# Crossbar transposes of softmax tiles: one per tile from 16 long rows, with the transposed tile kept in groups of 8 queries

## The chip, the core and the metric

The kernel runs on one NeuronCore of a Trainium2 chip. The metric is the device time of one execution in microseconds (us). The engines are TensorE (PE in the rows; PEld is its weight load), VectorE (DVE), ScalarE (ACT), GpSimd (POOL) and SyncE (SP), which here only issues DMAs.

## What is computed

Attention in which each row of scores keeps only what lies within `tau` of its maximum, and behind it a gated feed-forward layer with a three-tap convolution over the tokens:

```
q, k, v: (8, 8, 576, 64) float32;  x: (8, 576, 512) after the heads are joined
scores = q @ k^T / 8;  keep where scores >= max - tau;  attn = softmax(kept)
x = attn @ v
h = relu(x @ w_in)                         # 512 -> 1024
gate = sigmoid(three-tap convolution of h over the tokens)
out = (h * gate) @ w_out                   # 1024 -> 512
```

## The kernel before

**Tiling.** The 8 batches are cut into chunks of 256 and 320 tokens, 16 chunks in all; in a chunk the 8 heads are worked as four pairs of heads. A unit is one tile of 128 query rows (64 queries by two heads, or a leftover tile) against all 576 keys. Each unit computes scores on TensorE (`ps_s`, L569), the row maximum on VectorE (L581), the exponential on ScalarE (L588), the mask on VectorE (L591) and the normalisation on GpSimd (L629). The result is the tile `em`, 128 rows by 1152 float32.

**Two ways to transpose a tile.** The product with v wants `em` with the keys on the partitions, in the tile `eT`. For 53 of the units TensorE transposes blocks of 128 columns into PSUM (`ps_t`, L688) and ScalarE copies them into `eT` (L698 and L704). The other 91 units, all from the second batch on, go through the DMA crossbar (`cross`): ScalarE and GpSimd split the float32 words of `em` into their low and high 16 bits (`parts`, L337 and L339), SP writes `parts` to a DRAM buffer (`rows`, L666), and two DMA transposes per unit, one for each half of 64 queries, read `rows` and write `eT` (L673).

**The layout of eT before.** `eT` is `[128, 5, 9, 64]`: five groups of 64 queries, in each nine steps of keys, in each 64 queries side by side. There are two such buffers, and the two pairs of heads of one `attend` hold both; so the transposes for the next `attend` wait until the matmuls of this one have read them.

**attend** (L711 to L738) multiplies by v: nine steps, in each four matmuls whose moving operand is `eT[on, :w // D, step, :]` (`pa`, L724), `w` being 256 or 320 queries. There are 32 such groups of matmuls, 28 of them reading crossbar output. ScalarE and VectorE carry the result into `x` (L732, L735), on which the feed-forward layer works: `ph` (L754), a gate on ScalarE and VectorE, and `po` (L805). All these are full matmuls, 128 by 128; `ps_s` and `pa` are matmuls of 64 rows by 64 columns, four of which share the array.

**What sets the order.** No engine chooses at run time. `Plan.run` (L121) simulates all operations with a cost in ns for each, a priority, latencies and a cost for a change of the kind of matmul on TensorE (`SWITCH`, L46), and writes each engine's instructions in the order in which the simulation started them. An operation that `cross` declares with other costs or in another number can therefore move instructions on every engine. SP takes its DMAs strictly in the written order.

Of the kernel before, what the change touches and what calls it, by code (L numbers as in the profile page):

```python
# [10 lines left out]
F32 = mybir.dt.float32  # L11
# [4 lines left out]
U16 = mybir.dt.uint16  # L16
AF = mybir.ActivationFunctionType
# [37 lines left out]
FAR = 5  # L55
# [5 lines left out]
ETB = 2  # L61
# [3 lines left out]
LATE = {'load': 1357.0, 'copy': 18200.0, 'rows': 335.0, 'turn': -47.0}  # L65
# [22 lines left out]
class Plan:  # L88
# [13 lines left out]
    def op(self, engine, ns, fn, w=(), r=(), ahead=0.0, other=None, kind=None, late=0.0, port=False, ring=0.0):  # L102

        i = len(self.ops)
        before = set()
        for x in r:
            before.update(self.wrote[x])
            self.read.setdefault(x, set()).add(i)  # L110
        for x in w:
            before.update(self.wrote.get(x, ()))
            before.update(self.read.pop(x, ()))
            self.wrote[x] = (i,)
        before.discard(i)
        bufs = {x[0] for x in (*w, *r)}
        for x in bufs:
            x.left += 1
        self.ops.append((((engine, ns), *(other or ())), self.rank - ahead, fn if other is not None else lambda e: fn(), before, bufs, kind, late, port, ring))
# [135 lines left out]
def tile_tau_attention_gated_ffn(  # L255
# [13 lines left out]
    nc = tc.nc  # L269
    P = 128  # L270
    B, NP, _, _, S = qd.shape
    D = 64
# [4 lines left out]
    NBLK = 2 * S // P  # L277
# [6 lines left out]
    for b in range(B):  # L284
        for tiles in FIRST if not b else GROUPS:
# [4 lines left out]
                b=b, tiles=tiles, new=(o, end - o), cols=(a0, end - a0), tokens=(k0, (end if end == S else end - 1) - k0),  # L290
# [6 lines left out]
    wk = ctx.enter_context(tc.tile_pool(name="wk", bufs=2))  # L297
    sm = ctx.enter_context(tc.tile_pool(name="sm", bufs=4))
    far = ctx.enter_context(tc.tile_pool(name="far", bufs=FAR, space=bass.MemoryType.DRAM))
# [3 lines left out]
    plan = Plan()  # L303
# [49 lines left out]
    def act(n, psum=False):  # L353
        return n * 0.833 + (58 if psum else 95)
# [290 lines left out]
    def cross(u, em, dsts):  # L645

        parts = plan.buf(wk, "stage", STB, [P, 2 * S], U32, f"parts_{u}")

        def halves():
            return parts[:].bitcast(U16).rearrange("p (j k) -> p j k", j=2)  # L650

        rows = plan.buf(far, "rows", FAR, [2 * P, 2 * S], U16, f"rows_{u}")
        a = AHEAD["s"]
        for j in range(2):
            def part(e, j=j):
                src = em[:].bitcast(U16).rearrange("p (k two) -> p two k", two=2)[:, j]
                copy(e, halves()[:, j], src)

            choice = {"act": act(2 * S), "pool": pool1(2 * S), "dve": dve(2 * S)}
            home = ("act", "pool")[j]  # L660
            op(
                home, choice[home], part, w=[(parts, j)], r=[(em, 0), (em, 1)], ahead=a + AHEAD["parts"], port=True,
                other=[(e, ns) for e, ns in choice.items() if e != home]
            )
        put(
            864, lambda: nc.sync.dma_start(rows[:].rearrange("(q two) k -> q two k", two=2), halves()),  # L666
            w=[(rows, 0)], r=[(parts, 0), (parts, 1)], ahead=a, late=LATE["rows"]
        )
        for j in range(2):
            eT, g = dsts[j]  # L670

            def turn(j=j, eT=eT, g=g):
                nc.sync.dma_start_transpose(eT[:].bitcast(U16)[:, g], rows[j * P:(j + 1) * P, :])  # L673

            op("sp", 1560, turn, w=[(eT, (g, "x"))], r=[(rows, 0)], ahead=a, late=LATE["turn"], ring=1650)

    def transposes(u, em, dsts):

        def group(b0, n):

            pt = plan.buf(ps_t, "ps_t", 2, [P, 512], F32, f"ps_t_{u}_{b0}")

            def turns():
                for i in range(n):
                    block = em[:, (b0 + i) * P:(b0 + i + 1) * P]
                    nc.tensor.transpose(out=pt[:, i * P:(i + 1) * P], in_=block, identity=ident[:])  # L688

            op("pe", n * P * 0.852, turns, w=[(pt, 0)], r=[(em, 0), (em, 1), (ident, 0)], ahead=AHEAD["t"], kind="turn")  # L690

            def source():
                return pt[:, :n * P].rearrange("p (b g n) -> p g b n", b=n, g=2)

            if dsts[0][0] is dsts[1][0]:
                (eT, g), _ = dsts
                op(
                    "act", act(n * P, True), lambda: nc.scalar.activation(eT[:, g:g + 2, b0:b0 + n, :], source(), AF.Copy),  # L698
                    w=[(eT, (g, b0))], r=[(pt, 0)], ahead=AHEAD["t"] + AHEAD["evac"]
                )  # L700
            else:
                for j, (eT, g) in enumerate(dsts):
                    op(
                        "act", act(n * D, True), lambda j=j, eT=eT, g=g: nc.scalar.activation(eT[:, g, b0:b0 + n, :], source()[:, j], AF.Copy),  # L704
                        w=[(eT, (g, b0))], r=[(pt, 0)], ahead=AHEAD["t"] + AHEAD["evac"]
                    )

        for b0 in range(0, NBLK, BLOCKS):
            group(b0, min(BLOCKS, NBLK - b0))

    def attend(of, w, parts):  # L711

        pas = [plan.buf(ps_t, "ps_t", 2, [P, 512], F32, f"pa_{i}") for i, *_ in of]
        a = AHEAD["a"]
        read = parts + [(y[3], 0) for y in of]

        for step in range(NBLK):
            def mm(step=step):  # L720
                for (_, p, eT, vt, *_), pa in zip(of, pas):
                    for h in range(2):
                        j, on = h ^ p % 2, slice(h * D, (h + 1) * D)
                        nc.tensor.matmul(  # L724
                            pa[j * D:(j + 1) * D, :w], lhsT=vt[on, step, :], rhs=eT[on, :w // D, step, :],
                            start=(step == 0), stop=(step == NBLK - 1)
                        )

            op("pe", w * 4 / 2.4 + 6, mm, w=[(pa, 0) for pa in pas], r=read, ahead=a, kind="rows")
        for (i, p, eT, vt, x, off), pa in zip(of, pas):  # L730
            def high(pa=pa, x=x, off=off):
                nc.scalar.activation(x[:, 0, off:off + w], pa[:, :w], AF.Copy)  # L732

            def low(pa=pa, x=x, off=off):
                nc.vector.tensor_tensor(x[:, 1, off:off + w], pa[:, :w], x[:, 0, off:off + w].bitcast(F32), op=ALU.subtract)  # L735

            op("act", act(w, True), high, w=[(x, 0)], r=[(pa, 0)], ahead=a + AHEAD["low"])
            op("dve", dve(w), low, w=[(x, 1)], r=[(pa, 0), (x, 0)], ahead=a + AHEAD["low"])  # L738
# [121 lines left out]
    for now in range(len(units) + 1):  # L860
        plan.rank = float(now)
        if now < len(units):
# [4 lines left out]
            both = [i, i + 1] if n is None else [i]  # L867
            for x in both:
                if x not in eTs:
                    eTs[x] = plan.buf(wk, "eT", ETB, [P, 5, NBLK, D], F32, f"eT_{x}")  # L870
            if n is None:
                last = lasts[i]
                sides = [
# [96 lines left out]
```

## Time and profile before

| | |
|---|---|
| median of 3 runs | 833.04 us (832.44 to 833.35) |
| span of the profiled execution, first to last instruction | 832.4 us |
| TensorE busy | 810.5 us, 97% |
| VectorE, ScalarE, GpSimd busy | 722.3 (87%), 610.5 (73%), 496.4 us (60%) |
| granted TensorE clock | 1.000 of full speed throughout |
| share of 16 DMA engines of SP's queue | 76.5% |

Of the profiled execution the span alone is known; it lies 0.6 us under the median of the runs, and sums below are made on the span and carried to the median by that 0.6 us. Matmuls are pipelined and their ends are modelled, so TensorE's time is best read from the starts of its instructions, not from their lengths. A window row gives busy time with the number of instructions in brackets.

### The profile page before, as it was taken

How to read it: one execution, taken by the hardware profiler on the slowest of the kernel's cores; microseconds unless marked ns; L12 is line 12 of the kernel's file. 1: busy time of each engine (PE TensorE's matmuls, PEld its weight loads, DVE VectorE, ACT ScalarE, POOL GpSimd, SP SyncE). 2: the span in 40 equal slices, each digit the busy share in tenths (PEclk: the TensorE clock that was granted, in tenths of full speed). 3: DMA queues.
4: the chain of work that ended last, by engine and by line, in shares of the span. 5: the costliest groups of instructions: out<-in, count | busy, mean ns of one | idle time of the engine just before them, and what ended most of it. 6: DMA issues, size and time to landing. Idle time of an engine off the chain costs nothing.

```text
span 832.4 us, 20658 instructions
## 1 busy us (share of the span) xinstructions
PE 810.5 (97%) x7521; PEld 590.7 (71%) x7521; DVE 722.3 (87%) x1801; ACT 610.5 (73%) x1231; POOL 496.4 (60%) x639
## 2 busy tenths in 40 slices
PE   5899999999999999999999999999999999999998
PEld 2456667777677677767777677767778677777896
DVE  6999999989898799988989789997989979996542
ACT  5999787778777677877776777876767867776642
POOL 3477666855657466764666646774666647665321
PEclk9999999999999999999999999999999999999999
DMA  7544348899889878799998887889888988787200
GB/s 268 183 152 152 91 120 250 189 296 249 233 216 223 218 215 198 202 272 238 183 214 247 231 215 200 222 208 252 221 209 199 249 214 190 208 221 189 50 26 38
DMA packets 266133, 165.49 MB, mean 199 GB/s; under 512 B 220464, under 2 KB 239152, under 8 KB 266032
## 3 DMA queue, kind: packets, MB, share of 16 engines
q1 hardware_dynamic: 265600, 163.87, 76.5%
q8 instruction: 60, 0.98, 0.5%
q14 instruction: 41, 0.34, 0.1%
q10 hardware_dynamic: 432, 0.30, 0.1%
HBM read 47.34 MB, written 63.11 MB: 133 GB/s over the span
## 4 chain that ended last, share of the span: by engine, by line
PE 91%; ACT 4%; DVE 3%; POOL 1%; issue 1%; DMA 0%; POOLq 0%; DVEq 0%
PE ph L754 25%; PE po L805 25%; PE ps_s L569 19%; PE pa L724 16%; PE ps_t L688 6%; ACT em L588 1%; ACT eT L698 1%; DVE few L581 1%; DVE em L591 1%; POOL em L629 1%; POOL stage_f L402 1%; DMA k<-in_kp_dram 0%; DVE t L769 0%; ACT stage_f L389 0%; ACT w1h L410 0%
## 5 line engine op out<-in xcount | busy, mean ns | idle before, releaser
L629 POOL TENSOR_SCALAR em<-em,few 128x576 f32<-128x576 f32 x286 | 232.2, 823 | 182.2 <-DVE few L615 151.3
L588 ACT ACTIVATE em<-ps_s,few 128x576 f32<-128x576 f32 x288 | 209.9, 750 | 79.1 <-DVE few L581 64.1
L581 DVE TENSOR_REDUCE few<-ps_s 128x1 f32<-128x576 f32 x288 | 210.0, 748 | 42.6 <-PE ps_s L569 41.1
L591 DVE SCALAR_TENSOR_TENSOR em<-ps_s,few,em 128x576 f32<-128x576 f32 x288 | 224.1, 810 | 11.8 <-ACT em L588 4.9
L754 PE MATMUL ph<-x,w1h 128*128 128x322 f32 (+1 forms) x1024 | 232.4, 305 | 0.0
L754 PEld LDWEIGHTS ph<-x,w1h 128*128 128x128 f32 x1024 | 171.1, 189 | 23.2 <-issue 17.9
L344 POOL TENSOR_TENSOR gl<-t,gh 128x255 fp32r<-128x255 f32 (+9 forms) x192 | 121.3, 642 | 111.1 <-ACT gh L784 105.1
L569 PE MATMUL ps_s<-k,q 64*64 64x288 f32 x2048 | 164.6, 423 | 9.0 <-DVE k L341 4.3
L724 PE MATMUL pa<-eT,v 64*64 64x256 f32 (+1 forms) x2304 | 155.3, 404 | 0.7 <-ACT eT L698 0.7
L754 PE MATMUL ph<-x,w1l 128*128 128x322 f32 (+1 forms) x512 | 151.1, 295 | 0.0
L724 PEld LDWEIGHTS pa<-eT,v 64*64 64x64 f32 x2304 | 95.3, 133 | 47.5 <-issue 2.3
L805 PE MATMUL po<-w2h,gh 128*128 128x512 f32 x288 | 119.4, 415 | 0.0
L569 PEld LDWEIGHTS ps_s<-k,q 64*64 64x64 f32 x2048 | 67.1, 133 | 70.7 <-issue 32.1
L805 PE MATMUL po<-w2l,gh 128*128 128x512 f32 x288 | 112.7, 391 | 0.0
L805 PE MATMUL po<-w2h,gl 128*128 128x512 f32 x288 | 112.7, 391 | 0.0
L339 POOL COPY parts<-em 128x1152 uint16<-128x1152 uint16 x91 | 109.5, 1203 | 4.2
L337 ACT ACTIVATE parts<-em 128x1152 uint16<-128x1152 uint16 x91 | 106.5, 1170 | 3.2 <-POOL em L629 2.4
L769 DVE SCALAR_TENSOR_TENSOR t<-hp,cr 128x321 f32<-128x321 f32 (+1 forms) x128 | 87.8, 688 | 20.1 <-ACT hp L763 18.5
L754 PEld LDWEIGHTS ph<-x,w1l 128*128 128x128 f32 x512 | 96.5, 188 | 0.4
L776 ACT ACTIVATE t<-t,cm 128x321 f32<-128x321 f32 (+1 forms) x128 | 68.8, 539 | 24.7 <-DVE t L769 14.7
L769 DVE SCALAR_TENSOR_TENSOR t<-hp,cr,t 128x321 f32<-128x321 f32 (+1 forms) x128 | 85.5, 670 | 0.3
L688 PE MATMUL ps_t<-ident,em 128*128 128x128 f32 x477 | 74.0, 282 | 8.5 <-POOL em L629 3.3
(71 smaller groups left out, 832.9 us busy)
## 6 DMA issues: line engine op xcount, KB each, us to landing
rows<-parts SPq DMA_DIRECT2D x91, 576.0 KB, 3.9
q<-in_qd_dram SPq DMA_DIRECT2D x63, 256.0 KB, 4.0
v<-in_vc_dram SPq DMA_DIRECT2D x36, 288.0 KB, 4.6
out_dram<-ot SPq DMA_DIRECT2D x36, 256.0 KB, 3.9
k<-in_kp_dram SPq DMA_DIRECT2D x31, 288.0 KB, 5.1
stage<-in_w_in_dram SPq DMA_DIRECT2D x8, 512.0 KB, 5.7
stage<-in_w_out_dram SPq DMA_DIRECT2D x8, 512.0 KB, 4.0
eT<-rows SPq DMA_TRANSPOSE x182, 4.4
```

Of the source, the lines that this page charges most:

```text
L339: engines[e].tensor_copy(dst, src)
L344: engines[e].tensor_tensor(dst, x, y, op=ALU.subtract)
L569: nc.tensor.matmul(ps[g * D:(g + 1) * D, AT + c * CH:AT + (c + 1) * CH], lhsT=q(on, h), rhs=k[on, h * CH:(h + 1) * CH], start=True, stop=True)
L581: nc.vector.tensor_reduce(few[:, nm], scores(), op=ALU.max, axis=mybir.AxisListType.XY, negate=True)
L588: nc.scalar.activation(view(), scores(), AF.Exp, bias=few[:, nm])
L591: nc.vector.scalar_tensor_tensor(view(), scores(), few[:, th], view(), op0=ALU.is_ge, op1=ALU.mult, accum_out=few[:, total])
L629: engines[e].tensor_scalar(sl, sl, LEAST, few[:, 10 + h:11 + h], op0=ALU.add, op1=ALU.mult)
L688: nc.tensor.transpose(out=pt[:, i * P:(i + 1) * P], in_=block, identity=ident[:])
L724: nc.tensor.matmul(pa[j * D:(j + 1) * D, :w], lhsT=vt[on, step, :], rhs=eT[on, :w // D, step, :], start=(step == 0), stop=(step == NBLK - 1))
L754: nc.tensor.matmul(ph[:, :an], lhsT=w1[w][:, cb, fs], rhs=xs[cb][:, h, :an], start=(cb == 0 and i == 0), stop=(cb == NCB - 1 and i == 2))
L769: nc.vector.scalar_tensor_tensor(t[:, :kn], hp[:, o + k:o + kn + k], cr[:, j, f:f + 1], y, op0=ALU.mult, op1=ALU.add)
L805: nc.tensor.matmul(po[:], lhsT=x[:, f, at:at + P], rhs=w[:, f, :], start=(f == 0 and i == 0), stop=(f == NFB - 1 and i == 2))
```

## The change

`rows` becomes `[16, 18432]` 16-bit words instead of `[256, 1152]`. The tile's 128 query rows are written as 16 groups of 8: row `2 i + j` of DRAM holds, for query `i` of every group and half-word `j`, the groups' 1152 words one behind the other. A partition's two half-words, which stood side by side in DRAM (one piece of 4608 bytes), are now two pieces of 2304 bytes, 36,864 bytes apart. One DMA transpose takes the whole tile where two took a half each; its output runs in pieces of 16 words, which are 8 queries. `eT` becomes `[128, 40, 9, 8]`: 40 groups of 8 queries. ScalarE's copies from PSUM write the same layout, and the moving operand of `pa` is read as 32 or 40 runs of 8 queries. The costs told to the planner for the transposes are the same per tile (3120 ns on SP against 2 x 1560, 3296 ns of the ring against 2 x 1650).

```diff
-        rows = plan.buf(far, "rows", FAR, [2 * P, 2 * S], U16, f"rows_{u}")
+        rows = plan.buf(far, "rows", FAR, [16, P // 8 * 2 * S], U16, f"rows_{u}")
...
         put(
-            864, lambda: nc.sync.dma_start(rows[:].rearrange("(q two) k -> q two k", two=2), halves()),
+            864, lambda: nc.sync.dma_start(rows[:].rearrange("(i j) (g k) -> g i j k", j=2, g=P // 8), halves()),
             w=[(rows, 0)], r=[(parts, 0), (parts, 1)], ahead=a, late=LATE["rows"]
         )
-        for j in range(2):
-            eT, g = dsts[j]
-
-            def turn(j=j, eT=eT, g=g):
-                nc.sync.dma_start_transpose(eT[:].bitcast(U16)[:, g], rows[j * P:(j + 1) * P, :])
-
-            op("sp", 1560, turn, w=[(eT, (g, "x"))], r=[(rows, 0)], ahead=a, late=LATE["turn"], ring=1650)
+        groups = [(0, 16, *dsts[0])] if dsts[0][0] is dsts[1][0] else [(j * 8, 8, *dsts[j]) for j in range(2)]
+        for at, n, eT, g in groups:
+            def turn(at=at, n=n, eT=eT, g=g):
+                out = eT[:, g * 8:g * 8 + n].bitcast(U16).rearrange("p g b i -> p (g b) i")
+                nc.sync.dma_start_transpose(out, rows[:, at * 2 * S:(at + n) * 2 * S])
+
+            op("sp", 195 * n, turn, w=[(eT, (x, "x")) for x in range(g, g + n // 8)], r=[(rows, 0)], ahead=a, late=LATE["turn"], ring=206 * n)
...
             def source():
-                return pt[:, :n * P].rearrange("p (b g n) -> p g b n", b=n, g=2)
+                return pt[:, :n * P].rearrange("p (b g i) -> p g b i", b=n, i=8)
...
-                    "act", act(n * P, True), lambda: nc.scalar.activation(eT[:, g:g + 2, b0:b0 + n, :], source(), AF.Copy),
+                    "act", act(n * P, True), lambda: nc.scalar.activation(eT[:, g * 8:g * 8 + 16, b0:b0 + n, :], source(), AF.Copy),
...
-                            pa[j * D:(j + 1) * D, :w], lhsT=vt[on, step, :], rhs=eT[on, :w // D, step, :],
+                            pa[j * D:(j + 1) * D, :w], lhsT=vt[on, step, :], rhs=eT[on, :w // 8, step, :],
...
-                    eTs[x] = plan.buf(wk, "eT", ETB, [P, 5, NBLK, D], F32, f"eT_{x}")
+                    eTs[x] = plan.buf(wk, "eT", ETB, [P, 5 * D // 8, NBLK, 8], F32, f"eT_{x}")
```

All 91 crossed units take the first branch of `groups`, one transpose each. The written order shows the following.

On SP, the transposes for one `attend` ahead of its matmuls (`rows` is the DRAM buffer, `eT` the tile for one pair of heads; `x2` joins two instructions). Before:

```order
L673 DMA_TRANSPOSE eT_4026<-rows_3879 128x9x128 x2
L673 DMA_TRANSPOSE eT_4026<-rows_3945 128x9x128 x2
L673 DMA_TRANSPOSE eT_4123<-rows_4011 128x9x128 x2
L545 DMA v_3810<-in_vc_dram 128x576
L813 DMA out_dram<-ot_3749 128x512
```

The same place of the change, told with the tiles' new numbers:

```order
L673 DMA_TRANSPOSE eT_4000<-rows_3853 128x144x16
L673 DMA_TRANSPOSE eT_4000<-rows_3919 128x144x16
L673 DMA_TRANSPOSE eT_4089<-rows_3985 128x144x16
```

Six transposes have become three, in the same place of SP's order. Of SP's list only a few `rows` writes and loads move by a place or two.

On TensorE, the rows ahead of the first matmul that reads these transposes (`ps_s` are scores, `ph` and `po` the feed-forward layer, `pa` the product with v). Before:

```order
L569 MATMUL ps_s_0_4188<-k_3403,q_3962 64x288 x4
L569 MATMUL ps_s_1_4200<-k_3403,q_3962 64x288 x4
L754 MATMUL ph_0_4168<-x_3448,w1h 128x322
L754 MATMUL ph_0_4168<-x_3448,w1l 128x322
L754 MATMUL ph_0_4168<-x_3448,w1h 128x322
L805 MATMUL po_4131<-w2h,gh 128x512
L805 MATMUL po_4131<-w2h,gl 128x512
L805 MATMUL po_4131<-w2l,gh 128x512
L754 MATMUL ph_0_4168<-x_3451,w1h 128x322
L754 MATMUL ph_0_4168<-x_3451,w1l 128x322
L754 MATMUL ph_0_4168<-x_3451,w1h 128x322
L724 MATMUL pa_4223<-eT_4026,v_3810 64x256 x2
```

The same place of the change:

```order
L569 MATMUL ps_s_0_4159<-k_3382,q_3936 64x288 x4
L569 MATMUL ps_s_1_4171<-k_3382,q_3936 64x288 x4
L724 MATMUL pa_4178<-eT_4000,v_3776 64x256 x2
L724 MATMUL pa_4181<-eT_4089,v_3794 64x256 x2
L724 MATMUL pa_4178<-eT_4000,v_3776 64x256 x2
L724 MATMUL pa_4181<-eT_4089,v_3794 64x256 x2
```

Nine feed-forward matmuls that stood ahead of the first `pa` now stand behind the group. Up to this place, the 1202nd of 3545 rows, TensorE's list reads alike before and after, and so do its last 750 rows. Of the 28 `pa` groups that read crossbar output, five come clearly earlier behind the group before them (this is the first of them), six come later, and the others stay. Over the whole list the kind of matmul (64-row matmuls, transposes, full matmuls) changes 416 times before and 426 times after: the changes from full to 64-row matmuls go from 121 to 127, those back from 99 to 105, and between full matmuls and transposes there is one less each way. The waits on DMA semaphores that TensorE's rows carry fall from 257 to 173. VectorE, ScalarE and GpSimd have the same instructions as before, in nearly the same order.

## Rows read from the trace of the kernel before

**Rows 1.** Busy time by stage: PE, PEld, DVE, ACT, POOL; clock, DMA, GB/s.

```profile
20.00:111.00 91.00, 83.15 (x766) 52.55 (x763) 87.14 (x223) 84.76 (x180) 59.50 (x63) 1.00 0.44 139
111.00:785.00 674.00, 672.25 (x6448) 494.01 (x6447) 603.33 (x1512) 497.09 (x993) 420.42 (x541) 1.00 0.87 217
```

**Rows 2.** TensorE's waits, 111 to 785 us: total us, times, longest.

```profile
PE ps_t L688 <- POOL em L629: 0.8, 1, 0.8
PE ps_s L569 <- PE po L805: 0.5, 2, 0.3
```

**Rows 3.** DMA issues of the page: KB each, median us from issue to landing.

```profile
rows<-parts SPq DMA_DIRECT2D x91, 576.0 KB, 3.9
...
k<-in_kp_dram SPq DMA_DIRECT2D x31, 288.0 KB, 5.1
```

**Rows 4.** Transposes on SP's queue: ns held, min/median/max; landing.

```profile
L673 SPq DMA_TRANSPOSE eT<-rows x182: 1263/1574/2802, 118.7 to 770.8; - x182
...
DMA to landing us min/median/max: 3.6/4.4/6.6
```

**Rows 5.** All engines in a stretch that holds six transposes: DMA share, GB/s last.

```profile
401.00:411.70 10.70, 10.70 (x92) 8.76 (x85) 10.62 (x26) 8.09 (x18) 6.76 (x8) 1.00 1.06 172
```

**Rows 6.** SP's timeline, 300 to 372 us: start, length, DMA, how many.

```profile
306.16 9.49 SPq L673 DMA_TRANSPOSE eT<-rows  x6
...
359.78 7.18 SPq L673 DMA_TRANSPOSE eT<-rows  x4
```

**Rows 7.** TensorE's timeline ahead of a group of pa, 317 to 324 us.

```profile
317.63 0.40 PE L805 MATMUL po<-w2l,gh 128*128 128x512 f32 x1
317.96 1.20 PE L569 MATMUL ps_s<-k,q 64*64 64x288 f32 x16
319.09 0.41 PE L754 MATMUL ph<-x,w1h 128*128 128x322 f32 x1
...
319.64 0.39 PE L805 MATMUL po<-w2h,gh 128*128 128x512 f32 x1
319.87 0.39 PE L805 MATMUL po<-w2h,gl 128*128 128x512 f32 x1
...
320.63 0.31 PE L754 MATMUL ph<-x,w1h 128*128 128x322 f32 x1
320.87 2.82 PE L724 MATMUL pa<-eT,v 64*64 64x256 f32 x48
```

**Rows 8.** TensorE's timeline through a group of pa, 299 to 308 us.

```profile
300.08 1.20 PE L569 MATMUL ps_s<-k,q 64*64 64x288 f32 x16
301.10 5.03 PE L724 MATMUL pa<-eT,v 64*64 64x320 f32 x72
305.95 1.15 PE L569 MATMUL ps_s<-k,q 64*64 64x288 f32 x16
```

**Rows 9.** TensorE's timeline at the pa behind SP's second four transposes.

```profile
370.85 0.72 PE L724 MATMUL pa<-eT,v 64*64 64x320 f32 x8
```

**Rows 10.** The tightest group: SP's timeline, 722 to 730 us.

```profile
724.46 2.95 SPq L673 DMA_TRANSPOSE eT<-rows  x2
```

**Rows 11.** TensorE's timeline just ahead of that group, 726 to 730 us.

```profile
727.63 0.46 PE L754 MATMUL ph<-x,w1h 128*128 128x322 f32 x2
727.93 0.31 PE L754 MATMUL ph<-x,w1l 128*128 128x322 f32 x1
728.08 0.66 PE L754 MATMUL ph<-x,w1h 128*128 128x322 f32 x2
728.58 0.31 PE L754 MATMUL ph<-x,w1l 128*128 128x322 f32 x1
...
729.42 0.43 PE L724 MATMUL pa<-eT,v 64*64 64x256 f32 x2
```

**Rows 12.** ScalarE by line and shape: busy us, mean ns, idle before.

```profile
L698 ACT ACTIVATE eT<-ps_t 128x384 f32<-128x384 f32 x111 | 52.6, 514 | 8.7 <-PE ps_t L688 8.4
...
L763 ACT ACTIVATE hp<-ph 128x322 f32<-128x322 f32 x64 | 28.1, 439 | 10.2 <-PE ph L754 7.6 <-DVE t L774 1.8 <-DVE few L615 0.6
```

More of the change, by code (lines that the diff above doesn't have):

```diff
@@ L703, in group @@
                     op(
-                        "act", act(n * D, True), lambda j=j, eT=eT, g=g: nc.scalar.activation(eT[:, g, b0:b0 + n, :], source()[:, j], AF.Copy),
+                        "act", act(n * D, True), lambda j=j, eT=eT, g=g: nc.scalar.activation(eT[:, g * 8:g * 8 + 8, b0:b0 + n, :], source()[:, j * 8:j * 8 + 8], AF.Copy),
                         w=[(eT, (g, b0))], r=[(pt, 0)], ahead=AHEAD["t"] + AHEAD["evac"]
```

## Prediction

> **What bounds the kernel now.** I read the busy time by stage first, then TensorE's waits, then the timelines. From 111 to 785 us, the stage in which the crossbar is used, TensorE is busy for 672 of 674 us at the full clock, while VectorE is busy for 603, ScalarE for 497 and GpSimd for 420 [rows 1]. The reader is to see in the waits that almost nothing is waited for there: the two longest entries are 0.8 us and 0.5 us, and no DMA stands among them [rows 2]. So a transfer that lands earlier can give back next to nothing, and one that lands later is seen only when its reader has caught up with it. The DMA engines are busy too, 87% of that stage [rows 1] and 106% by the records in a stretch with six transposes, at 172 GB/s [rows 5]. The transposes are therefore a stream of bytes on full DMA engines and not a row of latencies. Before 111 us no crossbar runs, and ScalarE (85 of 91 us) is nearly as full as TensorE [rows 1].
>
> How near a transfer is to its reader is read from two timelines. The transposes for one `attend` start at 306.16 us and hold SP for 9.49 us, that is until 315.65 [rows 6]. The last of the six goes out one sixth of that earlier, at about 314.1. Landing comes 3.6 to 6.6 us after issue, 4.4 in the median [rows 4], so here at about 318.5. The first `pa` starts at 320.87 [rows 7], 2.4 us later. The tightest group has its last pair of transposes from 724.46 for 2.95 us [rows 10], the last issue at about 725.9, its landing between 729.5 and 730.3 by the least and the median; its `pa` starts at 729.42 [rows 11]. There the margin is nil already.
>
> **The change, part by part.**
>
> *The transposes.* 182 of them, each holding SP for 1574 ns in the median [rows 4], become 91 of twice the size. As the DMA engines are full while they run [rows 5], I take the bytes to decide: six took 9.49 us on SP [rows 6], three of twice the size take the same, and the last lands where it did. Lower bound: the long rows let the engines move what they moved in the whole stage with other transfers mixed in, 217 GB/s [rows 1], instead of 172; 9.5 us become 7.5. Upper bound: every half takes the longest hold seen, 2802 ns [rows 4], and six halves take 16.8 us. I take the middle, nearest to the median row. The Trainium skill, page "DMA: Bandwidth & Descriptors", section "Latency and other measured facts", gives a DMA transpose 261 GB/s, and about 350 to 400 where it is contiguous. The trace does not agree for the form of before, at 172 GB/s; by the page's upper figures six halves (1.77 MB) would take an estimated 5 us, and the group below with its margin gone would have it back.
>
> *The write of `rows`.* The same 576 KB, in pieces of 2304 instead of 4608 bytes. Loads of k come in pieces of 2304 bytes, and their 288 KB take 5.1 us to land where the 576 KB of `rows` take 3.9 [rows 3]. Bounds: nothing, or 1.2 us later per unit. The transposes of a group wait first for the matmuls of the `attend` before, so this later landing lies under that wait; I take nothing. Without that cover it would be up to 1.2 us at each of 28 groups.
>
> *The runs of 8 queries in `pa`.* 72 `pa` records of 320 queries take 4.85 us from start to start [rows 8]; each matmul is recorded twice and four run side by side, so a pass of four takes 4.85/18 = 0.269 us, 0.84 ns a query, in runs of 64. The scores of 288 keys in one run: 16 records, four passes, in 1.02 us [rows 8], a pass 0.255 us, 0.89 ns a key. Runs of 64 cost nothing against one run of 288, so I take nothing for runs of 8. Upper bound: a break costs one element's time, 1 in 8 more.
>
> *ScalarE's copies into `eT`.* 384 elements take 514 ns in six runs of 64, 322 in one run take 439 [rows 12]: 62 elements more for 75 ns, no sign that a run costs. I take nothing; upper bound an eighth more, 64 ns on each of 111, 7 us, of which only those before 111 us, where ScalarE is nearly full [rows 1], could show.
>
> *Six more changes each way between full and 64-row matmuls.* From `po` at 317.63 to the scores at 317.96 is 0.33 us, from one `po` to the next 0.23 (319.64, 319.87) [rows 7]: entering costs 0.10. The 16 score records take 1.13 us up to the next full matmul [rows 7] and 1.02 up to `pa` [rows 8]: leaving costs 0.11. Six pairs are 6 x 0.21 = 1.3 us, less up to 0.1 for the transposes' one change less: **1.2 us**. Nothing hides this, since TensorE is the engine that is full. Bounds: 0.6 us (half of the changes fall where TensorE pauses anyway) and 1.3 us.
>
> *Five `pa` groups that come earlier.* In the place that the order shows, the nine feed-forward matmuls between scores and `pa` fall away: `pa` would start 1.02 us after the scores, at 318.98 instead of 320.87 [rows 7, 8]. Against a landing at about 318.5 the margin falls from 2.4 to 0.5 us. Priced in the same way, the five groups come 1.1 to 3.8 us earlier. The one at 370.85 [rows 9], 1.6 us earlier, is due at 369.3; the last four transposes for it hold SP from 359.78 for 7.18 us [rows 6], the last goes out at 365.2 and lands at about 369.6: 0.3 us short. I allow **0.3 us** over the five together. Bounds: 0 (the transposes go faster) and 5 us (each lands a microsecond late). Behind a late `pa` stands everything on TensorE; after it, the next transposes are late too, since they wait for its reading of `eT`.
>
> *84 waits on DMA semaphores less on TensorE.* The first `pa` of a group, with several of them, starts 0.24 us after a `ph` (320.63 to 320.87) [rows 7] where the next `ph` starts after 0.15 (727.93 to 728.08) [rows 11]: 0.09 more, which is no more than the 0.10 of a change of kind. So the waits ran ahead; I take nothing, at most 0.01 us each, 0.8 us.
>
> Sum: 832.4 + 1.2 + 0.3 = 833.9 us of span, and with the 0.6 us around it **834.5 us**.
>
> **The rivals.**
>
> *The small pauses fall away (faster).* TensorE's records hide pauses: `ph` goes from 728.08 to 728.58 where the pair before took 0.30 us [rows 11], 0.20 us lost. Fewer semaphores and earlier landings could spare some. To be 1.7 us faster in spite of the 1.5 above it takes 16 such pauses; with 20 the time is 833.0 + 1.5 - 4.0 = 830.5. For it: the order is new over more than a thousand rows. Against: none of these pauses is tied to a DMA [rows 2].
>
> *The transposes get slower (slower).* 16 rows that lie 36,864 bytes apart are read at once. It decides from some 25% on: a group's 9.5 us grow by the margin of 2.4 us [rows 4, 6, 7]. At a third more, 3.2 us, the 28 groups lose 0.8 each, 22 us, and the time is 856. For it: the engines are full [rows 5], so any loss is passed on. Against: the same bytes are moved, in the same place of the queue.
>
> *The short runs cost (slower).* One element's time for every 8: 0.269/8 = 34 ns on each pass of 320 queries [rows 8], 27 on 256; 18 passes in 32 groups make 17 us, and the time is 851. For it: no row shows a run shorter than 64 on this path. Against: runs of 64 cost nothing. The Trainium skill, page "SBUF — State Buffer", section "Door 1: The DMA port swizzle", says that SBUF has lines of 16 bytes and that a crossing is paid for unless a line is hit at least twice. By that rule 8 queries are two full lines of four hits, and nothing is lost; no run here shows runs under 64.
>
> *The change does nothing it says,* the same packets at the same pace: that is the transposes' middle value, and lies in the forecast.
>
> **How the numbers follow.** A measurement of this kernel tells about 0.2%, 1.7 us, from no change. The forecast has 0.62: likeliest 834.5, its own range 832.5 to 837.5; since 834.5 lies just under the bound of 834.7, of the 0.62 I put 0.40 within 0.2%, 0.20 slower and 0.02 faster. The pauses have 0.16, all faster; slower transposes 0.08 and short runs 0.08, both slower; the 0.06 left, several small things that cancel, is the same. So faster 0.18, same 0.46, slower 0.36. The range reaches from 830.5, which takes in the pauses, to 841, which takes in the upper bounds of landings, writes and copies, and leaves out 0.16 above and a little below.
>
> **What would show it.** Right: TensorE's busy time within 2 us of before; 91 transposes with a hold near 3.1 us each and groups of three near 9.5 us; `pa` at 0.84 ns a query; ScalarE's copies within 20 ns of 514. The waits of TensorE would name `pa` behind a DMA for under 1 us. Wrong: a DMA wait of `pa` over 3 us, a pass of 320 queries over 0.28 us, or a TensorE that is idle less by 2 us than before. My weakest step is the pace of the transposes, which no row of long rows shows.

## Result and profile after

| | before | change |
|---|---|---|
| median on the same chip | 833.19 us (832.44 to 835.02, 4 runs) | 837.63 us (837.29 to 839.09, 4 runs) |
| ratio, 95% interval | | 1.0057 (1.0041 to 1.0072) |
| span of the profiled execution | 832.4 us | 837.3 us |
| TensorE busy | 810.5 us | 813.6 us |
| share of 16 DMA engines of SP's queue | 76.5% | 71.9% |
| DMA packets | 266,133 | 66,660 |

The change is 0.57% slower: 4.4 us by the medians, 4.9 us by the two profiled spans. That lies inside the range, 3.1 us above the likeliest time, and 0.1 us above the forecast's own part of it, 832.5 to 837.5.

The page of the changed kernel: packets and bytes of all DMAs, and the write of `rows` (KB, median us to landing), which answers to [rows 3].

```profile
DMA packets 66660, 165.47 MB, mean 198 GB/s; under 512 B 7888, under 2 KB 26576, under 8 KB 65104
...
rows<-parts SPq DMA_DIRECT2D x91, 576.0 KB, 5.0
```

The DMA side did change its form: a quarter of the packets for the same bytes. `rows` lands 1.1 us later than before.

SP's holds by line, for the tile `rows` (min/median/max ns), answering to [rows 4]; first the write of `rows` in before, then the two lines of the change:

```profile
L666 SPq DMA_DIRECT2D rows<-parts x91: 332/354/1261, 111.6 to 760.6; - x91
```

```profile
L666 SPq DMA_DIRECT2D rows<-parts x91: 557/566/1782, 111.6 to 766.0; - x91
L673 SPq DMA_TRANSPOSE eT<-rows x91: 2319/2966/4922, 118.8 to 774.9; - x91
```

A whole tile holds SP for 2966 ns where two halves held it for 2 x 1574 = 3148 ns, 6% less in the median. The sum over the kernel is the same, 294.3 against 294.5 us, because the long holds became more frequent: taken from the first half's start to the second's end, a tile held SP for over 4 us 4 times in 91 before, and 16 times now.

Busy time by stage, columns as in [rows 1]:

```profile
111.00:785.00 674.00, 669.90 (x6391) 486.51 (x6393) 601.73 (x1508) 495.40 (x988) 417.78 (x537) 1.00 0.81 217
```

The DMA engines are freer in the crossbar's stage, 0.81 for 0.87, while TensorE is idle there for 4.1 us instead of 1.8. The clock is full, so the clock is not the cause.

TensorE's waits from 111 to 785 us (total us, times, longest), answering to [rows 2]:

```profile
PE ps_s L569 <- issue: 1.4, 2, 0.7
PE ps_t L688 <- POOL em L629: 0.8, 1, 0.8
PE ps_s L569 <- PE ph L754: 0.5, 2, 0.3
PE pa L724 <- DMA eT<-rows: 0.5, 1, 0.5
PE ps_s L569 <- DVE em L591: 0.5, 1, 0.5
```

In before the list had the two rows of [rows 2] and one more:

```profile
PE ps_s L569 <- DVE em L591: 0.2, 1, 0.2
```

So two rows are new, 1.4 us of scores `ps_s` for which the view names no releaser ("issue") and 0.5 us of `pa` behind a DMA, and one has grown, scores behind VectorE's mask. Most of this is not DMA at all. The list adds up to 3.7 us, against 1.5 us before.

The parts that were costed at nothing, read where the forecast read them. SP's timeline at the first moved group answers to [rows 6]:

```profile
306.00 9.65 SPq L673 DMA_TRANSPOSE eT<-rows  x3
```

TensorE's timeline through a `pa` of 320 queries answers to [rows 8], and at the moved group to [rows 7]:

```profile
299.85 1.28 PE L569 MATMUL ps_s<-k,q 64*64 64x288 f32 x16
300.92 5.05 PE L724 MATMUL pa<-eT,v 64*64 64x320 f32 x72
305.76 1.18 PE L569 MATMUL ps_s<-k,q 64*64 64x288 f32 x16
306.87 0.39 PE L754 MATMUL ph<-x,w1h 128*128 128x256 f32 x1
...
317.39 0.39 PE L805 MATMUL po<-w2h,gl 128*128 128x512 f32 x1
317.62 0.40 PE L805 MATMUL po<-w2l,gh 128*128 128x512 f32 x1
317.95 1.20 PE L569 MATMUL ps_s<-k,q 64*64 64x288 f32 x16
318.97 3.39 PE L724 MATMUL pa<-eT,v 64*64 64x256 f32 x52
```

From start to start the 72 records take 4.84 us, where they took 4.85: runs of 8 queries cost nothing. The moved group starts at 318.97, within 0.01 us of the worked-out 318.98, and waits for nothing. A change of kind has kept its price: 0.33 us from `po` to the scores (317.62 to 317.95) for 0.23 from one `po` to the next, so 0.10 to enter, and 1.11 us from scores to `ph` (305.76 to 306.87) for 1.02 from scores to `pa`, so 0.09 to leave. ScalarE's copies, answering to [rows 12]:

```profile
L698 ACT ACTIVATE eT<-ps_t 128x384 f32<-128x384 f32 x111 | 52.5, 508 | 9.6 <-PE ps_t L688 9.1
```

**Where the time went.** I compared the start of each of the 32 `pa` groups in TensorE's timelines of the two kernels:

| start before, us | start after, us | later by |
|---|---|---|
| 301.1 | 300.9 | -0.2 |
| 343.9 | 344.6 | 0.7 |
| 395.9 | 397.3 | 1.4 |
| 494.2 | 495.7 | 1.5 |
| 564.8 | 566.6 | 1.8 |
| 589.2 | 590.2 | 1.0 |
| 612.3 | 616.3 | 4.0 |
| 632.0 | 636.7 | 4.7 |
| 687.8 | 693.7 | 5.9 |
| 777.5 | 782.7 | 5.2 |

Up to 301 us and again from 397 to 494 us, where TensorE's list reads alike, nothing is lost. The loss comes in two stretches, 320 to 397 and 590 to 690 us, both among places where the list was rewritten.

The first two of the new pauses are in TensorE's timeline near 366 and 370 us (start, length; in brackets the idle time before and who ended it):

```profile
365.86 0.39 PE L805 MATMUL po<-w2l,gh 128*128 128x512 f32 x1
366.87 1.50 PE L569 MATMUL ps_s<-k,q 64*64 64x288 f32 x16 [0.62 <-issue]
...
369.59 0.39 PE L805 MATMUL po<-w2l,gh 128*128 128x512 f32 x1
370.46 0.72 PE L569 MATMUL ps_s<-k,q 64*64 64x288 f32 x8 [0.48 <-DVE em L591]
```

VectorE at the same time; `em<-ps_s,few,em` is the mask:

```profile
365.96 0.81 DVE L591 SCALAR_TENSOR_TENSOR em<-ps_s,few,em 128x576 f32<-128x576 f32 x1
...
369.48 0.82 DVE L591 SCALAR_TENSOR_TENSOR em<-ps_s,few,em 128x576 f32<-128x576 f32 x1
```

The scores are written to one of two PSUM buffers (`bufs=2`, one for each half of a unit), which the unit before holds until its mask has read it. That mask ends at 365.96 + 0.81 = 366.77, and the scores start at 366.87. The second pause is the same: a mask from 369.48 to 370.30, scores at 370.46. The view names "issue" for the first one; its releaser is seen only by laying the two timelines side by side. In before the two halves of the scores stood apart there, the second 2.2 us behind the first, and neither waited:

```profile
365.17 0.72 PE L569 MATMUL ps_s<-k,q 64*64 64x288 f32 x8
...
367.40 0.72 PE L569 MATMUL ps_s<-k,q 64*64 64x288 f32 x8
```

Both pauses go with the order of this stretch: they are there, 0.62 and 0.48 us long, in e5, which has it, and absent from e3 and e6, which have the order of before there.

The third pause, and the one wait for a transpose, in TensorE's timeline, with VectorE's mask behind them:

```profile
628.92 0.32 PE L754 MATMUL ph<-x,w1h 128*128 128x322 f32 x1
629.98 0.72 PE L569 MATMUL ps_s<-k,q 64*64 64x288 f32 x8 [0.74 <-issue]
...
662.94 0.72 PE L724 MATMUL pa<-eT,v 64*64 64x320 f32 x4
664.16 1.83 PE L724 MATMUL pa<-eT,v 64*64 64x320 f32 x20 [0.50 <-DMA eT<-rows]
```

```profile
629.05 0.82 DVE L591 SCALAR_TENSOR_TENSOR em<-ps_s,few,em 128x576 f32<-128x576 f32 x1
```

The 0.74 us has a mask of VectorE that runs from 629.05 to 629.87. The 0.50 us is the only place in the kernel where the forecast's own worry, a `pa` moved ahead of its transposes, came true in the waits. The group that the forecast named for it, the one at 370.85 us, starts at 370.96 without a wait.

The idle time in brackets goes by modelled ends; from start to start the pauses cost more. The step to the scores at 366.87 takes 1.01 us and that at 370.46 0.87, for 0.33 elsewhere; that at 629.98 takes 1.06, for the 0.24 of [rows 7] from `ph` to `pa`; and `pa` at 662.94 needs 1.22 us for one pass of 0.27. That is 0.68 + 0.54 + 0.82 + 0.95 = 3.0 us.

### The profile page after: what moved, and what is told of

The parts are those of the page before. It is cut to its first block, busy times and chain, and to the rows that moved or that the text cites. A ratio compares the mean times of both kernels' runs of the same rounds, so it can differ in the third digit from the quotient of the medians.

```text
span 837.3 us, 20507 instructions
## 1 busy us (share of the span) xinstructions
PE 813.6 (97%) x7521; PEld 587.1 (70%) x7521; DVE 722.1 (86%) x1801; ACT 610.9 (73%) x1231; POOL 495.6 (59%) x639
## 2 busy tenths in 40 slices
DMA packets 66660, 165.47 MB, mean 198 GB/s; under 512 B 7888, under 2 KB 26576, under 8 KB 65104
## 3 DMA queue, kind: packets, MB, share of 16 engines
q1 hardware_dynamic: 66128, 163.86, 71.9%
## 4 chain that ended last, share of the span: by engine, by line
PE 88%; ACT 4%; DVE 3%; DMA 2%; SPq 1%; issue 1%; POOL 1%; POOLq 0%; DVEq 0%; ACTq 0%
PE ph L754 25%; PE po L805 22%; PE ps_s L569 18%; PE pa L724 16%; PE ps_t L688 6%; ACT em L588 1%; DVE few L581 1%; ACT eT L698 1%; DVE em L591 1%; DMA stage<-in_w_in_dram 1%; DMA eT<-rows 1%; POOL em L629 1%; SPq L673 1%; PE pw_stage L415 0%; DMA k<-in_kp_dram 0%
## 5 line engine op out<-in xcount | busy, mean ns | idle before, releaser
L724 PEld LDWEIGHTS pa<-eT,v 64*64 64x64 f32 x2304 | 92.5, 133 | 51.2 <-issue 2.3
L769 DVE SCALAR_TENSOR_TENSOR t<-hp,cr 128x321 f32<-128x321 f32 (+1 forms) x128 | 85.8, 671 | 20.0 <-ACT hp L763 19.4
```

Of the source, the lines that this page charges most:

```text
L724: nc.tensor.matmul(pa[j * D:(j + 1) * D, :w], lhsT=vt[on, step, :], rhs=eT[on, :w // 8, step, :], start=(step == 0), stop=(step == NBLK - 1))
L769: nc.vector.scalar_tensor_tensor(t[:, :kn], hp[:, o + k:o + kn + k], cr[:, j, f:f + 1], y, op0=ALU.mult, op1=ALU.add)
```

## Experiments

Four questions were put: is it the order of the instructions or the form of the transfers (e1 to e3), is any new order slower (e4, e7, e8), do the places add up (e5, e6), and is the merged form worth something when more goes through the crossbar (e9 to e12). Every kernel computes the whole reference. What each theory is, its expectation says. All times below are against the kernel before on the same chip.

**Order or form.** The first (e1) keeps the change's layout but transposes each tile in two halves and tells the planner so, which restores the order of before on every engine.

```diff
-        groups = [(0, 16, *dsts[0])] if dsts[0][0] is dsts[1][0] else [(j * 8, 8, *dsts[j]) for j in range(2)]
+        groups = [(j * 8, 8, *dsts[j]) for j in range(2)]
...
-            op("sp", 195 * n, turn, w=[(eT, (x, "x")) for x in range(g, g + n // 8)], r=[(rows, 0)], ahead=a, late=LATE["turn"], ring=206 * n)
+            op("sp", 195 * n, turn, w=[(eT, (x, "x")) for x in range(g, g + n // 8)], r=[(rows, 0)], ahead=a, late=LATE["turn"], ring=1650)
```

> The layout of the change in full (16 long rows, eT in groups of 8 queries), but with two transposes per tile, one for each 64 queries; the planner is told what it was told before, and every engine's order is that of the kernel before. If the order alone costs (my theory): within 0.15% of the kernel before, 832 to 834 us. If the layout or the 16-row form of the transposes costs (rival): 835 to 838 us.

The second (e2) is the reverse: layout and two transposes of before, told to the planner as one operation, so that TensorE's list is that of the change.

```diff
-        for j in range(2):
-            eT, g = dsts[j]
-
-            def turn(j=j, eT=eT, g=g):
+        def turn():
+            for j, (eT, g) in enumerate(dsts):
                 nc.sync.dma_start_transpose(eT[:].bitcast(U16)[:, g], rows[j * P:(j + 1) * P, :])
 
-            op("sp", 1560, turn, w=[(eT, (g, "x"))], r=[(rows, 0)], ahead=a, late=LATE["turn"], ring=1650)
+        op("sp", 3120, turn, w=[(eT, (g, "x")) for eT, g in dsts], r=[(rows, 0)], ahead=a, late=LATE["turn"], ring=3296)
```

> Nothing of the layout: the kernel before, with its two transposes of 128 rows, but told to the planner as one operation of 3120 ns and 3296 ns of the ring. Every engine's order is that of the changed kernel. If the order alone costs: 836.5 to 838.5 us, 0.4 to 0.7% slower than before. If the layout or form costs: 833 to 834.5 us.

The third (e3) is the change in full, one transpose per tile, told as two operations of which the first issues it and the second nothing; the order is that of before.

```diff
+        for j in range(2):
+            eT, g = dsts[j]
...
+            def turn(j=j, eT=eT, g=g):
+                if j == 0:
+                    at = dsts[0][1] * 8
+                    out = eT[:, at:at + 16].bitcast(U16).rearrange("p g b i -> p (g b) i")
+                    nc.sync.dma_start_transpose(out, rows[:])
...
-            op("sp", 195 * n, turn, w=[(eT, (x, "x")) for x in range(g, g + n // 8)], r=[(rows, 0)], ahead=a, late=LATE["turn"], ring=206 * n)
+            op("sp", 1560, turn, w=[(eT, (g, "x"))], r=[(rows, 0)], ahead=a, late=LATE["turn"], ring=1650)
```

> The change in full, one transpose per tile, but told to the planner as two operations of which only the first issues it: the order of the kernel before on every engine. If the order alone costs: 832 to 834 us. If one transpose of twice the size lands later than its reader can wait (rival): 835 to 838 us, with a wait of pa behind a DMA in TensorE's waits.

| | order | transposes | median us | ratio, 95% interval |
|---|---|---|---|---|
| before | old | two halves | 832.42 | |
| e1 | old | two halves, new layout | 832.89 | 1.0005 (0.9997 to 1.0014) |
| e3 | old | one, new layout | 832.98 | 1.0008 (0.9999 to 1.0017) |
| e2 | new | two halves, old layout | 837.41 | 1.0063 (1.0051 to 1.0076) |
| change | new | one, new layout | 837.63 (against 833.19) | 1.0057 (1.0041 to 1.0072) |

The waits of TensorE in e2, from 111 to 785 us, with not one byte of the new layout in it:

```profile
PE ps_s L569 <- issue: 1.4, 2, 0.7
PE ps_t L686 <- POOL em L629: 0.8, 1, 0.8
PE ps_s L569 <- PE ph L752: 0.5, 2, 0.3
PE ps_s L569 <- DVE em L591: 0.5, 1, 0.5
```

They are the waits of the change, less the 0.5 us of `pa`. The holds of the transposes in e1 and in e3, both in the order of before:

```profile
L673 SPq DMA_TRANSPOSE eT<-rows x182: 1109/1370/3363, 118.2 to 769.6; - x182
```

```profile
L677 SPq DMA_TRANSPOSE eT<-rows x91: 2377/2951/6182, 118.4 to 768.3; - x91
```

Two halves hold SP for 2 x 1370 = 2740 ns in the new layout, against 3148 in the old one, and the merged tile for 2951: the layout made the hold shorter, and merging took half of that back; in the sum over the kernel all of it (294.5 us before, 278.7 in e1, 295.1 in e3). The packets too fell with the layout, to 71,029 in e1, and by little more with the merging, to 66,660. The order alone makes the whole loss; layout, long rows and merging cost 0.1% or nothing.

**Is any new order slower?** The kernel before (e4), with 1648 ns of the ring told for each half instead of 1650. TensorE's list differs from before in 180 rows, with 429 changes of kind for 416.

```diff
-            op("sp", 1560, turn, w=[(eT, (g, "x"))], r=[(rows, 0)], ahead=a, late=LATE["turn"], ring=1650)
+            op("sp", 1560, turn, w=[(eT, (g, "x"))], r=[(rows, 0)], ahead=a, late=LATE["turn"], ring=1648)
```

> The kernel before with one number of the planner's changed: 1648 instead of 1650 ns of the ring for a transpose. No instruction's work changes; TensorE's order differs in 180 rows and has 429 changes of kind instead of 416. If a new order costs as such: 834.5 to 838 us. If the loss belongs to the order that merging makes: 832 to 834.5 us.

834.5 us, ratio 1.0024 (1.0014 to 1.0033): two nanoseconds in a planner's number cost 2.1 us. Two more draws, this time of the change itself (e7 with `ring=205 * n`, e8 with `ring=207 * n` for `206 * n`):

> The change in full, with 3280 ns of the ring told for a transpose instead of 3296. TensorE's order is a third one: it leaves both others at row 700, differs from before in 240 lines of the comparison and from the change in 172, and has 426 changes of kind as the change has. Theory A, an order is a draw, and what counts are a few places where scores follow their masks too closely: another time, anywhere from before less 1 to before plus 5 us, not tied to the 4.7 us of the change. Theory B, one operation of twice the length makes worse orders by itself: before plus 4 to 6 us again.

> The change in full, with 3312 ns of the ring told instead of 3296. TensorE's order leaves both others at row 728, differs from before in 164 lines of the comparison and from the change in 344, and has 425 changes of kind. Theory A, a draw: nearer to before than to the change, as its order is, before plus 0 to 3 us. Theory B, one operation of twice the length makes worse orders by itself: before plus 4 to 6 us.

The first gave 837.75 us, 1.0059 (1.0047 to 1.0071), the second 834.24 us, 1.0018 (1.0009 to 1.0026). So an order from one operation need not cost 5 us; but of the four other orders so far, the change's among them, none was as good as that of before. TensorE's waits in the second:

```profile
PE ps_s L569 <- PE po L805: 0.8, 2, 0.5
PE ps_t L688 <- POOL em L629: 0.8, 1, 0.8
```

They are no longer than before's (1.6 us against 1.5), the changes of kind are 9 more, and the time is 1.5 us more; the run with 1648 ns has 2.1 us for 13. By quotient that is 0.17 and 0.16 us for a change, but the timelines price one at 0.09 to 0.10, so 0.6 to 0.9 us of each run is something else that was not traced.

**Do the places add up?** One transpose per tile throughout; the planner is told of one operation only for some units, of two for the others (e6 with the condition reversed). TensorE's list then differs from before in one stretch alone.

```diff
+        if u < 72:
+            op("sp", 3120, turn, w=[(eT, (g, "x")) for eT, g in dsts], r=[(rows, 0)], ahead=a, late=LATE["turn"], ring=3296)
+        else:
+            for j, (eT, g) in enumerate(dsts):
+                op("sp", 1560, turn if j == 0 else none, w=[(eT, (g, "x"))], r=[(rows, 0)], ahead=a, late=LATE["turn"], ring=1650)
```

> One merged transpose per tile everywhere. The planner is told of one operation for the first 72 units and of two halves, as before, for the other 72. TensorE's order is that of the change up to row 1451 of 3545 and that of before from there on; it differs from before only from row 1205 to row 1451, some 320 to 397 us. Theory A, the loss is the sum of the places where the order differs: the product with v that follows this stretch came 1.4 us late in the change (397.3 against 395.9 us) and stays so, so before plus 1.4 us, ratio about 1.0017, with the two pauses of the scores behind VectorE's masks near 366 and 369 us. Theory B, the later places are late because the plan was already out of step in the first stretch: most of the loss comes with it, before plus 3 to 5 us. Theory C, the first stretch is made good later where SP or VectorE has slack: before plus 0 to 0.5 us.

> The reverse: two halves told for the first 72 units, one operation for the other 72. TensorE's order is that of before up to row 2075 and from row 2769 on, and that of the change between, some 514 to 690 us. Theory A: the rest of the loss, 4.4 to 4.9 less 1.4, so before plus 3.0 to 3.5 us, ratio 1.0036 to 1.0042, with the pause of the scores near 628 us and that of the product with v near 662 us. Theory B: little, before plus 0 to 1.5 us. Theory C: all of it, 4.4 to 4.9 us.

833.73 us, 1.0015 (1.0006 to 1.0024), and 837.24 us, 1.0059 (1.0047 to 1.0071), against 832.71. The early stretch costs 1.0 us, the late one 4.5; theory A had 1.4 and 3.0 to 3.5. The early loss is not the seed of the later one, which B would have. Whether part of it is made good later is not settled: the late value is too high for A by 1.0 to 1.5 us and lies in C's 4.4 to 4.9, while the early one, 1.0 us with an interval from 0.5 to 2.0, lies above C's 0 to 0.5. In the early run TensorE has one change of kind fewer than before (counted in the traces), and its waits come to 2.5 us, 1.0 more than before's; two of the five rows:

```profile
PE ps_s L569 <- issue: 0.6, 1, 0.6
PE ps_s L569 <- DVE em L591: 0.5, 1, 0.5
```

So there the scores behind their masks are about the whole loss. The waits of the late run, which has the pause of 0.75 us behind a mask and not these two:

```profile
PE ps_s L569 <- DMA q<-in_qd_dram: 2.1, 2, 1.7
...
PE ps_s L569 <- issue: 0.7, 1, 0.7
PE pa L731 <- DMA eT<-rows: 0.4, 1, 0.4
```

The 1.7 us stands at 233 us, in the part whose list is that of before, and e3, with the same list there, has no such wait: this execution had a late load. Its span of 838.5 us less these 2.1 is 836.4. It took 840.33 us, and the other five 836.28 to 837.29, so the late load is that one execution's and does not explain the median; the excess stays open.

**More through the crossbar.** Seven more units, one in each chunk of 256 tokens from the second batch on, in the merged form told as two halves (e9), and in the old form with the same order (e10):

```diff
-CROSS = ((2, 1, 2, 1), (2, 2, 2, 1), (0, 0))
+CROSS = ((2, 1, 2, 2), (2, 2, 2, 1), (0, 0))
```

> Seven more units go through the crossbar (98 for 91; the last pair of heads of each chunk of 256 tokens has two crossed units for one), in the layout and the merged form of the change, but told to the planner as two halves. TensorE loses 63 transposes, 63 x 0.095 us (six took 0.57 us from start to start at 334.66 us of the trace before) = 6.0 us, and has 441 changes of kind for 416, 25 x 0.1 = 2.5 us more. Theory A, only the order and TensorE's own work count: before minus 3 us, less what a new order costs in pauses (0 to 4 us), so before minus 3 to plus 1 us, and the same as the next kernel within 0.1%. Theory B, the merged form leaves the DMA engines room (72% for 76% of the span): this kernel is faster by 2 us or more than the next one, which has the same order in the old form.

> The same 98 crossed units and the same order on every engine, in the layout and with the two transposes of before. Theory A: as the kernel above within 0.1%. Theory B: 2 us or more slower than it, with waits of the product with v for its transposes in the middle stage.

849.01 us, 1.0193 (1.0172 to 1.0213), and 845.63 us, 1.0157 (1.0143 to 1.0171), against 832.49. Both theories fell: no gain at all, and the merged form is the slower one, by 3.4 us of the medians (846.05 to 851.25 in five runs, against 844.63 to 846.85 in four). Where the 13 us of the halves went was not traced; their listed waits come to 6.7 us, 5.2 more than before's. The waits for transposes, merged first:

```profile
PE pa L728 <- DMA eT<-rows: 4.0, 4, 1.6
```

```profile
PE pa L724 <- DMA eT<-rows: 0.5, 1, 0.5
```

The difference is 3.5 us, of 3.4 between the medians and 4.7 between the two profiled spans. SP's timeline of the merged form ahead of the longest of these waits, and the wait in TensorE's:

```profile
336.89 4.35 SPq L677 DMA_TRANSPOSE eT<-rows  x1
...
341.97 4.97 SPq L677 DMA_TRANSPOSE eT<-rows  x1
...
348.38 5.00 SPq L677 DMA_TRANSPOSE eT<-rows  x1
```

```profile
356.96 0.43 PE L728 MATMUL pa<-eT,v 64*64 64x256 f32 x2 [1.64 <-DMA eT<-rows]
```

And SP's timeline of the halves at the same place:

```profile
335.53 4.30 SPq L673 DMA_TRANSPOSE eT<-rows  x2
...
340.55 3.17 SPq L673 DMA_TRANSPOSE eT<-rows  x2
...
345.07 4.56 SPq L673 DMA_TRANSPOSE eT<-rows  x2
```

The first tile starts 1.4 us later in the merged form and the third 3.3 us later: two tiles that hold SP for 4.35 and 4.97 us where pairs of halves held it for 4.30 and 3.17, and a `rows` that lands 5.2 us after its issue instead of 4.0. Over the kernel 27 of 98 tiles hold SP for more than 4 us, against 10 of 98. Which of the two, the later `rows` or the longer hold, does more was not taken apart. The last two runs tell the planner of one operation, as the change does (e11), or take the seven units from another pair of heads, told as two (e12):

```diff
-CROSS = ((2, 1, 2, 1), (2, 2, 2, 1), (0, 0))
+CROSS = ((2, 2, 2, 1), (2, 2, 2, 1), (0, 0))
```

> The 98 crossed units in the merged form, told as one operation, as the change does: 425 changes of kind for 416 of before. Theory A: before minus 6.0 plus 0.9 us, less pauses of 0 to 4 us of a new order: before minus 5 to minus 1 us. Rival, one operation of twice the length makes orders with late scores by itself: 4 us or more above the first kernel of these.

> As the first of these, but the seven units are taken from the second pair of heads of each chunk of 256 tokens: 430 changes of kind. Theory A: before minus 6.0 plus 1.4 us, less pauses of 0 to 4 us: before minus 4.6 to minus 0.6 us. Rival, 98 crossed units load the DMA engines or ScalarE and GpSimd, which split the words, too much: slower than before, with waits of the product with v for its transposes.

854.44 us, 1.0265 (1.0248 to 1.0281), and 853.45 us, 1.0254 (1.0237 to 1.0271). The expected gains of up to 5 us turned into losses of 21 to 22 us, as both rivals had it, but their reasons are not shown. Told as one operation the same work is 5.4 us slower than told as two (849.01), and the rival's late scores are little of it: scores behind masks went from 1.6 us only to 2.1, `pa` behind transposes from 4.0 to 5.8. Part of it is, by an estimate, the granted clock, which is full in the profiled execution of e9. In e11, columns as in [rows 1], and the wait in TensorE's timeline:

```profile
745.00:750.00 5.00, 3.02 (x26) 1.76 (x28) 3.80 (x10) 3.40 (x6) 4.46 (x7) 0.76 0.73 201
750.00:755.00 5.00, 5.00 (x56) 3.61 (x52) 1.10 (x3) 0.74 (x1) 1.22 (x3) 0.56 0.63 210
```

```profile
748.34 3.25 PE L724 MATMUL pa<-eT,v 64*64 64x256 f32 x26 [1.98 <-DMA eT<-rows]
```

In these 10 us, in the first half of which TensorE waits for 1.98 us, the clock goes from its upper level (2.4 GHz) to its lower (1.2 GHz) and back, and is full again from 755 us; the two shares leave out 1.2 + 2.2 = 3.4 us of the full clock, an estimate of what it cost that execution. All four executions show a mean clock below full, 0.995 to 0.998. The last kernel has 4.2 us of `pa` behind transposes beside 5.4 us of scores behind masks; that the crossed units load the engines too much is not shown by it, since from 111 to 785 us the DMA engines' share is 0.85 there, under the 0.87 of e9, and ScalarE and GpSimd are about as busy (488 and 423 us, for 487 and 427). With e8 beside it, one operation is not always this much worse; it was worse in both pairs tried. No kernel tried beats the one of before.

## Why the prediction was right or wrong

**Inside the range, in part by luck.** The room above 837.5 us was made for late landings, writes and copies, and little of it was used for them (0.95 us at one `pa`); scores that wait for their masks, 2.0 us, are in no term of the sum. No change within 0.2% had the larger chance, 0.46; the slower time that came had 0.36.

**Right.** That the DMA side would give nothing and cost nothing in the order of before (e3: 1.0008), and that what counts is the order on a full TensorE. Groups of three transposes took 9.65 us for the forecast's 9.5, one transpose 2.97 for 3.1, a `pa` of 320 queries the same, the copies 508 ns for 514. The 84 waits fewer showed no gain. By the upper figures of the Trainium skill, page "DMA: Bandwidth & Descriptors", section "Latency and other measured facts", six halves would have taken an estimated 5 us; the trace does not agree for long rows either (1.77 MB in 9.65 us on SP, 183 GB/s; in before 1.77 MB in 9.49 us, 186 GB/s, where the 172 GB/s of the prediction are those of a whole stretch). The rule of lines of 16 bytes hit twice, from the Trainium skill, page "SBUF — State Buffer", section "Door 1: The DMA port swizzle", gives no loss for runs of 8; the trace agrees, at 4.84 us against 4.85, and no run here has shorter ones to test where the rule has a loss.

**Wrong: the step "Five `pa` groups that come earlier", 0.3 us.** It was mis-sized, and it looked at one wait only. I asked of each moved `pa` whether its transposes had landed; that cost 0.5 us of listed wait (0.95 from start to start) in one place, and not in the one that was worked out. But the planner moved everything around those groups, and what caught up with its producer was another instruction: scores on TensorE against the masks on VectorE that free their PSUM buffer. VectorE, 87% busy, stood in TensorE's waits before with 0.2 us, which [rows 2] leaves out, and became the releaser of the new pauses. Listed waits grew by 3.7 - 1.5 = 2.2 us.

**Right in size: the changes of kind,** 1.2 us. At 0.09 to 0.10 us a change in the changed kernel's timeline, the ten more cost 1.0 us. Of the 4.9 us between the spans, the four pauses are 3.0 from start to start, less the 0.2 that before had behind a mask, and the changes 1.0; the last 1.1 us was not placed. TensorE's idle time as a whole grew by only 1.8 us, from 21.9 to 23.7, and its busy time by 3.1, so part of the loss lies in records that read as busy, as the prediction said of such records.

**Right with its bound: the write of `rows`.** Its landing came 1.1 us later, near the bound of 1.2, and was hidden, as taken: e1 and e3 have it too and are within 0.1% of before. The price without that cover was not measured by itself; in the runs with 98 crossed units the later `rows` and the longer tiles together are 3.4 us.

**The rivals.** Slower transposes and short runs did not come. "The small pauses fall away" had it the wrong way round: the listed waits grew. "The change does nothing it says" was half true: the packets fell to a quarter, the pace did not move. TensorE's busy time grew by 3.1 us, more than the 2 us allowed, the one sign named for being right that failed; the sign that was missing from my list was a wait of the scores.

## What to carry to other kernels

Where a planner writes the order, an edit that tells it the same work in other pieces is first of all a new order: run the edit's form under the old order and the old form under the new order before judging either. In a kernel whose bound engine is never idle, look at every instruction that the new order moves closer to its producer, not only at the ones the edit is about; the PSUM buffers that another engine frees come first. Change the layout and the merging of a transfer one at a time: here the layout gave the fewer packets and the shorter holds, and merging gave the holds back.

## What the runs showed of the hardware

- Transposes from 16 long rows instead of 128: 71,029 packets in the kernel for 266,133 with two transposes per tile (e1), 66,660 with one. SP's queue took 74.2% and 72.2% (e3) of the DMA engines for 76.5%. One transpose per tile held SP as long in total as two from 128 rows (294.3 us in the change, 294.5 before).
- The write of 576 KB in pieces of 2304 instead of 4608 bytes holds SP for 566 ns (before: 354) and lands 5.0 us after its issue (before: 3.9).
- The halves of the new layout (e1) held SP for 1370 ns in the median, those of the old for 1574, a merged tile (e3) for 2951, and the time did not change.
- Matmuls that read their moving operand in runs of 8 float32 instead of 64 took the same: 72 records of 320 queries in 4.84 us for 4.85.
- In e11 the granted clock fell to 0.76 and 0.56 in two stretches of 5 us, the first of which holds a wait of TensorE of 1.98 us.
